# A late layernorm on ScalarE, mask work in three pieces, another order of q groups, and one attention step a unit later

## The chip, the cores and the metric

The kernel runs on one core of one Trainium2 chip. The metric is the device time of one execution in microseconds, the median of several runs. The kernel before took 277.28 us (three runs, 276.76 to 277.5).

The engines are named as in the profile: PE is TensorE (PEld its weight loads), DVE is VectorE, ACT is ScalarE, POOL is GpSimd, and SP is SyncE, which here issues the DMAs.

## The reference

One transformer block on a sequence of 2048 rows of width 640, in bf16: linear attention with a learned softmax feature map, then a gated feed-forward part. Layernorm has no scale and no bias.

```python
def _A_ref(x, wqkv, w_phi, wo):            # B, S, D = 1, 2048, 640;  H = 32 heads of Dh = 20
    q, k, v = ...                          # x @ wqkv, split into heads
    pq = jnp.einsum("bhsd,hdf->bhsf", q, w_phi)
    pk = jnp.einsum("bhsd,hdf->bhsf", k, w_phi)
    phi_q = jnp.concatenate([_softmax(pq), _softmax(-pq)], axis=-1)
    phi_k = jnp.concatenate([_softmax(pk), _softmax(-pk)], axis=-1)
    kv = jnp.einsum("bhsf,bhsd->bhfd", phi_k, v)
    z  = jnp.einsum("bhsf->bhf", phi_k)
    num = jnp.einsum("bhqf,bhfd->bhqd", phi_q, kv)
    den = jnp.einsum("bhqf,bhf->bhq", phi_q, z)[..., None] + 1e-6
    return (num / den).transpose(...).reshape(B, S, D) @ wo

def _B_ref(x, w_gate, w_up, w_down):       # F = 1536
    return (_gelu(x @ w_gate) * (x @ w_up)) @ w_down

h  = x + _A_ref(_layernorm(x), ...)
h2 = h + _B_ref(_layernorm(h), ...)
```

## The kernel before

**Tiles and batches.** The 2048 rows are 16 tiles of 128 rows (`t` = 0 to 15), in four batches `b` of four tiles. The width 640 is five chunks `c` of 128. PE's program order and SP's are those of the source; so are those of the other engines, each of which runs its own instructions in order and waits on semaphores for the others. A wait at the head of one engine's queue therefore holds all that stands behind it.

**The k and v phase** (source lines 411 to 505) goes over the tiles. For each tile: the layernormed rows, transposed, lie in `LN1T[b]` (640 columns on five chunks of partitions); `k_tile` multiplies them by Wk with the feature map already folded in (matrix `Wk2`, PSUM tile `pk`) and ACT makes the two exponentials, exp(pk) and exp(-pk), in `Ek[t]` (line 310); `v_mm` and `v_ev` make v for a tile four ahead (`vS`, a ring of eight; a column of ones beside v gives z). `k_norm` (line 313) normalises: DVE sums each head's exponentials (`sk`, line 317) and takes the reciprocal (`rs`, line 321); the two signs' `vt`, v times that reciprocal, are made on POOL (sign 1 always, sign 0 for the tiles of `VP` = 0, 2, 4, 6, 9, 11) and on DVE (sign 0 of the others, put off by one tile through `todo`). On DVE the order of one tile is thus sk(t), vt(t-1) where it is DVE's, rs(t). `kv_tile` multiplies `Ek` and `vt` into the accumulator `kvp`, 20 small matmuls a tile, in four batches: `KVG` = after the k matmuls of tiles 5, 9, 13 and 15; tiles 12 to 15 come last (lines 503 and 504). PSUM in this phase is three buffers of two banks and the two banks of `kvp`.

**Layernorm of tiles 0 and 1.** The first two tiles are handled apart: k and v are computed from the merely centred rows (`xc`), and the row factor rstd is put in by the scale operands of the exponentials and of the copy of v. Only q needs their full layernorm in `LN1T[0]`, so it is made late, in iteration 10: `ln_ap(0)` on DVE (line 144) and `ln_a(1)` on DVE (line 390), each followed by a DMA transpose on SP's queue (line 155). `ln_ap(t, on_act=True)` would make the same on ACT (line 139), which needs `mr`, the mean times minus rstd, which tile 0's statistics (`ln_0`) do not compute. SP's next issues after these two transposes are the loads of Wg, Wo and Wu in iteration 13 (lines 499 to 501).

**POOL's KV work.** In iteration 9, behind that tile's `vt`, POOL clears `KV` (line 489), builds the mask `kmask` of the head blocks (lines 490 to 495: a memset and four affine selects, each pair on one half of the partitions) and copies it into the two columns of `KV` that stand for z (lines 496 and 497). `KV` and `kmask` are wanted by `kv_mask`, after the last `kv_tile`: DVE and POOL multiply the accumulator by the mask into `KV` (line 355).

**The q phase.** q is computed transposed, 20 chunks of 128 columns by 512 rows, chunk number 5*b + c. `QG` lists how the chunks are grouped; a group of two fills one PSUM tile `pq` (`q_mm`, line 368, five matmuls of 512 columns a chunk) and ACT takes the two exponentials (`q_exp`, line 373). Four groups are done in iteration 15 of the k phase (`QT`), ahead of the last `kv_tile`s; the others in the order written out by hand in lines 739 to 781, between the attention steps of tiles 0 and 1. Attention of tile t wants the five chunks of its batch.

**Attention steps.** `attn_a` multiplies phi_q by KV (PSUM tiles `ab`, line 546, two PSUM buffers a tile) and copies the result out (`AB`, line 566, ACT or DVE); `attn_b`, `attn_b2`, `attn_b3` make the quotient (`pr`, `den`, `w` on POOL or DVE; `rd`, `tt`, `o` on DVE) and send `o` through a DMA transpose; `attn_c` multiplies by Wo (`po`, line 618); `attn_d`, `attn_d2`, `attn_e` add the residual, take the second layernorm and transpose it to `LN2T`.

**The feed-forward units.** From 90 us on a unit is `gate_up` (ten matmuls into one PSUM buffer `gu`, line 678; gelu on ACT, line 681; product `GT` on DVE, line 684) or `down` (`pd`, line 697). `weave(units, stages)` runs the units in order and puts each attention step in front of the unit whose number it was given; `attn_at(t, i, offs)` gives the eight steps of tile t the numbers i + offs. In the first weave, tile 3 has i = 1 and its `attn_a` stands in front of unit 2. PSUM is here four buffers of two banks, and a new tile takes the buffer that was released first in the source's order; `attn_a` copies its halves in the order (1, 0) for tile 5 and (0, 1) for the others, which sets which of its two buffers is released first.

Of the kernel before, what the change touches and what calls it, by code (L numbers as in the profile page):

```python
# [10 lines left out]
ALU = mybir.AluOpType  # L11
# [6 lines left out]
def kernel(  # L18
# [12 lines left out]
    nc = tc.nc  # L31
# [17 lines left out]
    LQ = (7, 8, 9, 9, 10)  # L49
    FQ = (10, 11, 12, 13, 14)  # L50

    QG = ((0, 1), (2, 3), (4, 5), (6,), (7, 8), (9, 10), (11, 12), (13, 14), (15,), (16,), (17,), (18,), (19,))
    QT = (15, 15, 15, 15)
    T3 = 3

# [20 lines left out]
    x_sb = [const.tile([P, 4, D], BF16, name=f"x_sb{b}") for b in range(NB)]  # L76
# [5 lines left out]

    Eq = [const.tile([P, len(g), 2, 512], BF16, name=f"Eq{j}") for j, g in enumerate(QG)]
    ident = const.tile([P, P], BF16, name="ident")
# [6 lines left out]
    def eq(t, c, s):  # L91
        for E, g in zip(Eq, QG):
            if t // 4 * NC + c in g:
                return E[:, g.index(t // 4 * NC + c), s, t % 4 * P:(t % 4 + 1) * P]

    def small(pool, shape, name, bufs=3):
        return pool.tile(shape, F32, name=name, bufs=bufs)

    def gtile(name):
        return psG.tile([P, 2, 512], F32, name=name, tag="G")  # L100

    def ln_stats(pool, tiles, tag, act=True, between=None, log=False):

        n = len(tiles)
        mv = small(pool, [P, n, nc.vector.BN_AGGR_DIM], "mv" + tag)
        stats = small(pool, [P, n, 2, nc.vector.BN_STATS_DIM], "stats" + tag)
        for j, xt in enumerate(tiles):
            for i in range(2):
                nc.vector.bn_stats(stats[:, j, i, :], xt[:, i * HD:(i + 1) * HD])
                if between and i == j == 0:  # L110
                    between()
        for j in range(n):
            nc.vector.bn_aggr(mv[:, j, :], stats[:, j])
        ve = small(pool, [P, n], "ve" + tag)
        rstd = small(pool, [P, n], "rstd" + tag)
        if log is not False:

            def root():
                nc.scalar.activation(ve, mv[:, :, 1], ACTF.Ln, bias=eps)
                nc.scalar.activation(rstd, ve, ACTF.Exp, scale=-0.5)  # L120

            if log is True:
                root()
            else:
                log.append(root)
        else:
            nc.gpsimd.tensor_scalar_add(ve, mv[:, :, 1], EPS)
            nc.gpsimd.tensor_tensor(rstd, ve, nhalf[:, 0:n], op=ALU.pow)

        mr = small(pool, [P, n], "mr" + tag)  # L130
        if act:
            for j in range(n):
                nc.gpsimd.tensor_scalar(mr[:, j:j + 1], mv[:, j, 0:1], rstd[:, j:j + 1], -1.0,
                                        op0=ALU.mult, op1=ALU.mult)
        return [(xt, mv[:, j, 0:1], rstd[:, j:j + 1], mr[:, j:j + 1]) for j, xt in enumerate(tiles)]
# [11 lines left out]
    def transpose_to(dst, src, on_pe, on_dve=False):  # L147

        if on_pe:
            tp = psG.tile([P, 16, P], BF16, name="tp", tag="G")  # L150
            for c in range(NC):
                nc.tensor.transpose(tp[:, c, :], src[:, c * P:(c + 1) * P], ident)  # L152
            (nc.vector.tensor_copy if on_dve else nc.scalar.copy)(dst, tp[:, 0:NC, :])  # L153
        else:
            nc.sync.dma_start_transpose(dst, src)
# [7 lines left out]
    p1 = p1_cm.__enter__()  # L163
# [81 lines left out]
    lnp, Ek, Vt = {}, {}, {}  # L245

    CT = (0, 1)
    nrstd = [p1.tile([P, 1], F32, name=f"nrstd{t}") for t in CT]

    def ln_0(t):  # L250
        xt, mean, rstd, _ = lnp[t] = ln_stats(p1, [x_sb[0][:, t, :]], f"c{t}", False, None, True)[0]
        nc.gpsimd.tensor_scalar(nrstd[t], rstd, -1.0, None, op0=ALU.mult)
        xc = fp.tile([P, D], BF16, name="xc", bufs=2)
        nc.vector.tensor_scalar(xc, xt, mean, None, op0=ALU.subtract)
        return xc
# [5 lines left out]
    def ln_ap(t, on_act=False, on_pe=False):  # L261
        ln = (ln_act if on_act else ln_dve)(p1, "1", *lnp[t])
        if on_pe:
            lnp[t] = ln
        else:
            transpose_to(LN1T[t // 4][:, :, t % 4 * P:(t % 4 + 1) * P], ln, False)
# [38 lines left out]
    def k_tile(t):  # L305
        pk = gtile("pk")
        proj(pk, t, Wk2, rows=t == 0)
        Ek[t] = ev.tile([P, 2, D], BF16, name="E", bufs=8)
        for s in range(2):
            nc.scalar.activation(Ek[t][:, s, :].rearrange("p (u f) -> p u f", u=2), pk[:, :, 0:HD],  # L310
                                 ACTF.Exp, scale=((lnp[t][2], nrstd[t]) if t in CT else (1.0, -1.0))[s])
# [47 lines left out]
    def q_mm(j, part=(0, 1)):  # L359

        if 0 in part:
            pqs[j] = gtile("pq")
        for i, bc in enumerate(QG[j]):
            if i not in part:
                continue
            b, c = divmod(bc, NC)
            for kc in range(NC):
                nc.tensor.matmul(pqs[j][:, i, :], lhsT=Wq2[:, kc, c * P:(c + 1) * P], rhs=LN1T[b][:, kc, :],  # L368
                                 start=(kc == 0), stop=(kc == NC - 1))

    def q_exp(j, signs=(0, 1)):
        for s in signs:
            nc.scalar.activation(Eq[j][:, :, s, :], pqs[j][:, 0:len(QG[j])], ACTF.Exp, scale=(1.0, -1.0)[s])  # L373

# [82 lines left out]
    for t in range(NT):  # L457
        if t == T3:
            ps_cm.close()
            psG = ps_cm.enter_context(tc.tile_pool(name="psG", bufs=3, space=PSUM, reuse_waits="tile"))  # L460
            psK = ps_cm.enter_context(tc.tile_pool(name="psK", bufs=1, space=PSUM, reuse_waits="tile"))
            kvp = psK.tile([P, 2, 512], F32, name="kvp")
        k_tile(t)
        if t == 0:
            ln_ap(6)
        if t in FQ:
            fold(WqT, Wq2, True, [i for i, f in enumerate(FQ) if f == t])
        for j in range(len(QT)):
            if t == QT[j]:
                q_mm(j)  # L470
                q_exp(j)
        for i in KVG.get(t, ()):
            kv_tile(i)
        if 0 < t < NT - 4:
            v_mm(t + 4)
        if t > 0 and t + 6 < NT:
            ln_ap(t + 6, on_act=True)
        if 0 < t < NT - 4:
            v_ev(t + 4)
        if t % 2 == 0 and t + 8 < NT:  # L480
            ln_st(t + 8, t + 9)
        k_norm(t)
        load_T(WqT, 0, *[i for i, f in enumerate(LQ) if f == t])
        if t == 10:

            ln_ap(0)
            transpose_to(LN1T[0][:, :, P:2 * P], ln_a(1), False)
        if t == 9:
            nc.gpsimd.memset(KV, 0.0)
            nc.gpsimd.memset(kmask, 1.0)  # L490
            for r in HALF:
                nc.gpsimd.affine_select(out=kmask[r], in_=kmask[r], pattern=[[4, NC], [-Dh, 4]],
                                        compare_op=ALU.is_ge, fill=0.0, base=0, channel_multiplier=1)
                nc.gpsimd.affine_select(out=kmask[r], in_=kmask[r], pattern=[[-4, NC], [Dh, 4]],
                                        compare_op=ALU.is_ge, fill=0.0, base=Dh - 1, channel_multiplier=-1)
            nc.gpsimd.tensor_copy(KV[:, :, 0, :, KC - 1], kmask)
            nc.gpsimd.tensor_copy(KV[:, :, 1, :, 0], kmask)
        if t == 13:
            nc.sync.dma_start(Wg, wg_v)
            nc.sync.dma_start(Wo, wo_v)  # L500
            nc.sync.dma_start(Wu, wu_v)
# [60 lines left out]
    def attn_a(t, dve=0):  # L562
        attn_a_mm(t)
        AB, ab = ABs[t % 2], st[t, "ab"]
        for u in ((1, 0) if t in (5,) else (0, 1)):
            (nc.vector.tensor_copy if u >= 2 - dve else nc.scalar.copy)(
                AB[:, :, u * UH:(u + 1) * UH].rearrange("p s h f -> p s (h f)"), ab[u][:, :, 0:UH * KC])
        st[t] = AB
# [169 lines left out]

    q_mm(q)
    attn_a(0, 1)  # L740
    q_exp(q)
    q_mm(q + 1)
# [41 lines left out]
    def attn_at(t, i, offs):  # L784

        fns = (attn_a, attn_b, attn_b2, attn_b3, attn_c, attn_d, attn_d2, attn_e)
        return [(i + o, fn, t) for fn, o in zip(fns, offs) if o >= 0]

    SHORT = (0, 2, 3, 4, 9, 9, 10, 12)
    SHORT2 = (0, 2, 3, 4, 10, 10, 11, 13)  # L790
    LONG = (0, 1, 2, 5, 5, 6, 7)

    def attn_rest(t, i):
# [2 lines left out]


    weave(gus(0, 0, 256) + downs(0, (0, 1)),
          attn_at(2, 0, (-1, 0, 1, 2, 7, 7, 8, 10)) + attn_at(3, 1, (1, 2, 3, 4, 9, 9, 10, 12)) + attn_at(4, 6, SHORT2) + attn_at(5, 9, SHORT2) +
          attn_at(6, 13, SHORT2))  # L800
    weave(gus(0, 256, 512) + downs(0, (2, 3)),
          attn_at(7, 0, SHORT) + [(12, split), (14, attn_pair, 8), (16, attn_pair, 10)] + attn_rest(8, 15) +
# [37 lines left out]
```

## Time and profile before

| | |
|---|---|
| median of the runs | 277.28 us (276.76 to 277.5) |
| profiled execution | 277.27 us |
| its span, first to last instruction | 275.5 us |
| granted TensorE clock | 1.000 |
| PE busy | 270.3 us (98%) |
| DVE busy | 175.7 us (64%) |
| ACT busy | 140.2 us (51%) |
| POOL busy | 97.1 us (35%) |
| weight loads (PEld) busy | 173.6 us (63%) |
| DVE busy between 30 and 60 us | 9.79 + 9.90 + 9.79 us of 30 |

The busy shares are means over stages. The k and v phase lies between about 6 and 70 us, the q phase between 59 and 89.5 us, the woven feed-forward part after that. Matmuls are pipelined and their ends are modelled, so a busy PE is not yet a PE at its peak, and the starts of neighbouring instructions are the better measure there. Spans on POOL are rough. A line of the timeline gives the start in us, the duration in us, the engine, the source line, the operation, what it writes and reads, how many instructions are merged in it, and in brackets the idle time before them with what ended it. A line of the waits gives who waited for whom, the total in us, how many times, and the longest.

### The profile page before, as it was taken

The numbers are of one execution on the slowest core, as the hardware profiler recorded it, in microseconds if no ns is written. First come the engines' busy times: TensorE is split into PE (matmuls) and PEld (weight loads), VectorE is DVE, ScalarE is ACT, GpSimd is POOL, SyncE is SP. The second block draws the span as 40 slices with busy tenths as digits, with TensorE's granted clock in tenths as the row PEclk, the third lists the DMA queues.
The fourth block names the chain that finished last, engine by engine and source line by source line (L and its number), as shares of the span: only waits on it lengthen the run. The fifth ranks groups of instructions, "written<-read, shape, count | busy, mean of one in ns | idle before, by whom it ended". The sixth has DMA issues, their size and how long they took to land.

```text
span 275.5 us, 5939 instructions
## 1 busy us (share of the span) xinstructions
PE 270.3 (98%) x2345; PEld 173.6 (63%) x2345; DVE 175.7 (64%) x333; ACT 140.2 (51%) x241; POOL 97.1 (35%) x218
## 2 busy tenths in 40 slices
PE   7999999999899999999999999999999999999995
PEld 4777777765455887788764545675455576444574
DVE  5889999999495776675478773356866333333322
ACT  5789898869489755374552345223245510223100
POOL 4248897765202317365312553101165300000000
DMA  7963525589820021323111142110123111000011
GB/s 197 209 230 61 75 51 101 83 266 394 264 91 0 4 48 38 84 48 77 26 48 48 26 69 51 38 61 2 48 47 71 27 48 50 24 0 0 0 50 48
DMA packets 42235, 21.37 MB, mean 78 GB/s; under 512 B 35040, under 2 KB 40416, under 8 KB 42208
## 3 DMA queue, kind: packets, MB, share of 16 engines
q1 hardware_dynamic: 41552, 20.98, 30.1%
q8 instruction: 18, 0.29, 0.5%
q10 hardware_dynamic: 656, 0.03, 0.2%
q14 instruction: 9, 0.07, 0.1%
HBM read 10.18 MB, written 2.62 MB: 46 GB/s over the span
## 4 chain that ended last, share of the span: by engine, by line
PE 86%; issue 4%; DVE 4%; DMA 2%; ACT 1%; POOL 1%; SPq 0%; DVEq 0%; ACTq 0%; POOLq 0%
PE gu L678 37%; PE pd L697 19%; PE po L618 8%; PE pv L277 6%; PE pk L277 5%; PE pq L368 5%; PE ab L546 2%; DMA Wv<-in_A_wqkv_dram 2%; DVE sk L317 2%; DVE rs L321 1%; PE kvp L343 1%; PE tp L152 1%; POOL vt L325 1%; PE pv L293 1%; PE wa L232 1%
## 5 line engine op out<-in xcount | busy, mean ns | idle before, releaser
L681 ACT ACTIVATE g<-gu 128x512 bf16<-128x512 f32 (+1 forms) x60 | 30.7, 512 | 68.9 <-PE gu L678 68.7
L684 DVE TENSOR_TENSOR GT<-gu,g 128x512 bf16<-128x512 f32 (+1 forms) x60 | 34.5, 580 | 47.8 <-PE gu L678 39.2
L678 PE MATMUL gu<-LN2T,Wg 128*128 128x512 bf16 (+1 forms) x300 | 61.8, 337 | 0.0
L678 PE MATMUL gu<-LN2T,Wu 128*128 128x512 bf16 (+1 forms) x300 | 61.8, 337 | 0.0
L697 PE MATMUL pd<-Wd,GT 128*128 128x320 bf16 (+2 forms) x396 | 53.5, 295 | 0.0
L697 PEld LDWEIGHTS <-GT 128*128 128x128 bf16 x396 | 37.9, 98 | 14.7 <-DVE GT L684 0.2
L678 PEld LDWEIGHTS <-Wu 128*128 128x128 bf16 x300 | 29.4, 98 | 22.6
L678 PEld LDWEIGHTS <-Wg 128*128 128x128 bf16 x300 | 28.8, 98 | 21.4
L277 PEld LDWEIGHTS <-LN1T 128*128 128x128 bf16 x290 | 27.8, 98 | 10.5
L700 DVE TENSOR_TENSOR y<-pd,x_sb 128x320 bf16<-128x320 f32 (+2 forms) x29 | 13.9, 480 | 28.9 <-PE pd L697 28.9
L325 POOL TENSOR_TENSOR vt<-vS,rs 128x672 bf16<-128x672 bf16 x22 | 29.1, 1343 | 9.1 <-DVE rs L321 8.8
L618 PE MATMUL po<-Wo,oT 128*128 128x320 bf16 x160 | 24.3, 299 | 0.0
L277 PE MATMUL pk<-Wk,LN1T 128*128 128x320 bf16 x160 | 24.2, 299 | 0.0
L368 PE MATMUL pq<-LN1T,Wq 128*128 128x512 bf16 x100 | 23.1, 379 | 0.0
L317 DVE TENSOR_REDUCE sk<-E 128x64 f32<-128x1280 bf16 x16 | 22.9, 1430 | 0.0
L373 ACT ACTIVATE Eq<-pq 128x1024 bf16<-128x1024 f32 (+1 forms) x26 | 20.0, 830 | 1.7 <-PE pq L368 1.7
L618 PEld LDWEIGHTS <-oT 128*128 128x128 bf16 x160 | 15.6, 98 | 7.4 <-ACT oT L153 0.5
L310 ACT ACTIVATE E<-pk 128x640 bf16<-128x640 f32 x28 | 18.2, 707 | 3.8 <-PE pk L277 3.8
L277 PE MATMUL pv<-Wv,LN1T 128*128 128x320 bf16 x130 | 19.8, 299 | 0.0
L595 DVE TENSOR_TENSOR tt<-AB,w 128x1280 bf16<-128x1280 f32 x12 | 17.8, 1486 | 1.1 <-POOL w L588 0.9
L139 ACT ACTIVATE ln<-x_sb,v,rstd 128x640 bf16<-128x640 bf16 x14 | 12.9, 920 | 10.4 <-POOL v L657 10.0
L368 PEld LDWEIGHTS <-Wq 128*128 128x128 bf16 x100 | 9.4, 98 | 10.0
(114 smaller groups left out, 292.8 us busy)
## 6 DMA issues: line engine op xcount, KB each, us to landing
out_dram<-y SPq DMA_DIRECT2D x15, 160.0 KB, 1.8
Wg<-in_B_w_gate_dram SPq DMA_DIRECT2D x1, 1920.0 KB, 7.9
Wu<-in_B_w_up_dram SPq DMA_DIRECT2D x1, 1920.0 KB, 12.8
Wd<-in_B_w_down_dram SPq DMA_DIRECT2D x1, 1920.0 KB, 7.9
x_sb<-in_A_x_dram SPq DMA_DIRECT2D x2, 640.0 KB, 6.3
Wo<-in_A_wo_dram SPq DMA_DIRECT2D x1, 800.0 KB, 9.5
x_sb<-in_A_x_dram SPq DMA_DIRECT2D x4, 160.0 KB, 3.4
Wv<-in_A_wqkv_dram SPq DMA_DIRECT2D x2, 320.0 KB, 4.6
```

What stands on the lines that cost most here:

```text
L277: nc.tensor.matmul(ps[:, u, 0:HD], lhsT=lnT(t, c), rhs=W[:, c, u * HD:(u + 1) * HD], start=(c == 0), stop=(c == NC - 1))
L310: nc.scalar.activation(Ek[t][:, s, :].rearrange("p (u f) -> p u f", u=2), pk[:, :, 0:HD], ACTF.Exp, scale=((lnp[t][2], nrstd[t]) if t in C ...
L317: nc.vector.reduce_sum(sk, Ek[t].rearrange("p s (h f) -> p (s h) f", f=Dh), axis=AX.X)
L325: eng.tensor_tensor(vt[:, s], vS[t % 8], rs[:, s * H:(s + 1) * H, None].to_broadcast([P, H, VC]), ALU.mult)
L368: nc.tensor.matmul(pqs[j][:, i, :], lhsT=Wq2[:, kc, c * P:(c + 1) * P], rhs=LN1T[b][:, kc, :], start=(kc == 0), stop=(kc == NC - 1))
L373: nc.scalar.activation(Eq[j][:, :, s, :], pqs[j][:, 0:len(QG[j])], ACTF.Exp, scale=(1.0, -1.0)[s])
L595: nc.vector.tensor_tensor(tt.rearrange("p s (h f) -> p s h f", f=Dh), num, w[:, :, :, None].to_broadcast([P, 2, H, Dh]), ALU.mult)
L618: nc.tensor.matmul(pos[u], lhsT=st[t][:, c, :], rhs=Wo[:, c, u * HD:(u + 1) * HD], start=(c == 0), stop=(c == NC - 1))
L678: nc.tensor.matmul(gu[i][:, 0:n], lhsT=W[:, c, f * P:(f + 1) * P], rhs=LN2T[b][:, c, a0:a1], start=(c == 0), stop=(c == NC - 1))
L681: nc.scalar.activation(g[:, 0:n], gu[0][:, 0:n], ACTF.Gelu_apprx_tanh)
L684: nc.vector.tensor_tensor(st[b, "g", f][:, a0:a1], gu[1][:, 0:n], g[:, 0:n], ALU.mult)
L697: nc.tensor.matmul(ps, lhsT=st[b, "g", f][:, tl * P:(tl + 1) * P], rhs=Wd[:, f, f0:f1], start=(f == 0), stop=(f == NF - 1))
```

## The change

It has five edits.

- The first group of `QG` becomes (5, 6), two chunks of batch 1; (4,) stands alone in its place. There are still 13 groups, and the four groups of iteration 15 still hold chunks 0 to 6.
- `ln_0` makes `mr` for tile 0 on POOL, and `ln_ap(0)` moves from DVE in iteration 10 to ACT in iteration 12. In the order of instructions it stands on ACT behind the Wq copy of iteration 12 and ahead of tile 13's exponentials. On SP tile 1's transpose comes first and tile 0's second; both still stand ahead of Wg, Wo and Wu.
- POOL's KV work is split: the two memsets in iteration 7, the four selects in iteration 8, the two copies in iteration 10, each behind that tile's `vt`.
- In `attn_a` the copy order (1, 0) is for tile 4 and no longer for tile 5.
- `attn_a`, `attn_b`, `attn_b2` and `attn_b3` of tile 3 come one unit later; its `attn_a` now stands behind unit 2's `gate_up`. Its later steps stay.

```diff
-    QG = ((0, 1), (2, 3), (4, 5), (6,), (7, 8), ...)
+    QG = ((5, 6), (0, 1), (2, 3), (4,), (7, 8), ...)
...
     def ln_0(t):
-        xt, mean, rstd, _ = lnp[t] = ln_stats(p1, [x_sb[0][:, t, :]], f"c{t}", False, None, True)[0]
+        xt, mean, rstd, mr = lnp[t] = ln_stats(p1, [x_sb[0][:, t, :]], f"c{t}", False, None, True)[0]
         nc.gpsimd.tensor_scalar(nrstd[t], rstd, -1.0, None, op0=ALU.mult)
+        if t == 0:
+            nc.gpsimd.tensor_scalar(mr, mean, nrstd[0], None, op0=ALU.mult)
...
         if t == 10:
-            ln_ap(0)
             transpose_to(LN1T[0][:, :, P:2 * P], ln_a(1), False)
-        if t == 9:
+        if t == 12:
+            ln_ap(0, on_act=True)
+        if t == 7:
             nc.gpsimd.memset(KV, 0.0)
             nc.gpsimd.memset(kmask, 1.0)
+        if t == 8:
             for r in HALF:
                 nc.gpsimd.affine_select(out=kmask[r], in_=kmask[r], ...)
                 nc.gpsimd.affine_select(out=kmask[r], in_=kmask[r], ...)
+        if t == 10:
             nc.gpsimd.tensor_copy(KV[:, :, 0, :, KC - 1], kmask)
             nc.gpsimd.tensor_copy(KV[:, :, 1, :, 0], kmask)
...
-        for u in ((1, 0) if t in (5,) else (0, 1)):
+        for u in ((1, 0) if t in (4,) else (0, 1)):
...
-          attn_at(2, 0, (-1, 0, 1, 2, 7, 7, 8, 10)) + attn_at(3, 1, (1, 2, 3, 4, 9, 9, 10, 12)) + ...
+          attn_at(2, 0, (-1, 0, 1, 2, 7, 7, 8, 10)) + attn_at(3, 1, (2, 3, 4, 5, 9, 9, 10, 12)) + ...
```

More of the change, by code (lines that the diff above doesn't have):

```diff
@@ L50 @@
     FQ = (10, 11, 12, 13, 14)
-    QG = ((0, 1), (2, 3), (4, 5), (6,), (7, 8), (9, 10), (11, 12), (13, 14), (15,), (16,), (17,), (18,), (19,))
+    QG = ((5, 6), (0, 1), (2, 3), (4,), (7, 8), (9, 10), (11, 12), (13, 14), (15,), (16,), (17,), (18,), (19,))
     QT = (15, 15, 15, 15)
@@ L798 @@
     weave(gus(0, 0, 256) + downs(0, (0, 1)),
-          attn_at(2, 0, (-1, 0, 1, 2, 7, 7, 8, 10)) + attn_at(3, 1, (1, 2, 3, 4, 9, 9, 10, 12)) + attn_at(4, 6, SHORT2) + attn_at(5, 9, SHORT2) +
+          attn_at(2, 0, (-1, 0, 1, 2, 7, 7, 8, 10)) + attn_at(3, 1, (2, 3, 4, 5, 9, 9, 10, 12)) + attn_at(4, 6, SHORT2) + attn_at(5, 9, SHORT2) +
           attn_at(6, 13, SHORT2))
```

## The prediction

> **What bounds the kernel now.** I read the page's chain first, then who waited for whom on TensorE (PE), then the timeline around each of its stalls. The granted clock is 1.000 in the core view, so no part of this is a clock matter.
>
> ```profile
> PE 86%; issue 4%; DVE 4%; DMA 2%; ACT 1%; POOL 1%; SPq 0%; DVEq 0%; ACTq 0%; POOLq 0%
> ```
>
> The chain is PE almost throughout, so the ceiling of any scheduling edit is the time that PE stands still. The waits of PE name all of it:
>
> ```profile
> PE wu L214 <- PEq L824: 0.8, 1, 0.8
> PE kvp L343 <- POOL vt L325: 0.7, 1, 0.7
> PE pv L293 <- DMA Wv<-in_A_wqkv_dram: 0.5, 1, 0.5
> ```
>
> The first and third lie before 7 us and nothing in the diff reaches them. The second is the one at stake. Timeline around it (start, us, engine, line):
>
> ```profile
> 66.87 2.29 PE L343 MATMUL kvp<-vt,E 128*64 128x84 bf16 x110
> ...
> 67.79 0.86 DVE L325 TENSOR_TENSOR vt<-vS,rs 128x672 bf16<-128x672 bf16 x1
> 67.86 1.96 POOL L325 TENSOR_TENSOR vt<-vS,rs 128x672 bf16<-128x672 bf16 x1 [1.35 <-DVE rs L321]
> 69.87 0.38 PE L343 MATMUL kvp<-vt,E 128*64 128x84 bf16 x10 [0.71 <-POOL vt L325]
> ...
> 70.19 2.33 PE L368 MATMUL pq<-LN1T,Wq 128*128 128x512 bf16 x10
> ```
>
> PE's last ten phi_k@V matmuls wait for tile 15's second vt on POOL, done at 69.82. Matmul ends are modelled, so I size the stall by starts: 80 kvp matmuls took 42.00 to 43.66 (1.66), 40 took 30.14 to 31.03 (0.89), so 40 more cost 0.77 and these 120 should take 2.43; they took 66.87 to 70.19, 3.32. The stall is 0.89.
>
> Why POOL is late: from about 41 us on VectorE (DVE) runs sk, vt, rs for each tile with no idle time, tile 15's sk starting at 64.95 though its E was ready at 60.84. So any DVE time before 67 us moves the 69.82. The dear piece of that queue:
>
> ```profile
> 49.76 2.58 POOL L325 TENSOR_TENSOR vt<-vS,rs 128x672 bf16<-128x672 bf16 x2 [1.32 <-DVE rs L321]
> ...
> 51.53 1.81 DVE L144 TENSOR_SCALAR ln<-x_sb,mvc,rstdc 128x640 bf16<-128x640 bf16 x1
> ...
> 52.28 0.83 POOL L489 MEMSET KV<- 128x880 bf16 x1
> ...
> 53.27 0.43 DVE L390 TENSOR_SCALAR ln<-x_sb,va 128x640 bf16<-128x640 bf16 x1
> ...
> 53.62 1.47 DVE L317 TENSOR_REDUCE sk<-E 128x64 f32<-128x1280 bf16 x1
> ...
> 54.70 1.31 POOL L325 TENSOR_TENSOR vt<-vS,rs 128x672 bf16<-128x672 bf16 x1
> 55.01 1.72 DVE L325 TENSOR_TENSOR vt<-vS,rs 128x672 bf16<-128x672 bf16 x1
> ```
>
> The ln of tile 0 takes 1.81 here; the seven other L144 take 0.44 to 0.45. It finishes 1.00 after POOL's vt and 0.23 after the memset. DVE's vt at 55.01 takes 1.72 against 0.85 when POOL is idle, and ends 0.72 after POOL's vt; those at 45.09, 60.45, 63.66 and 66.30 end 0.71 to 0.72 after POOL's too. So such DVE operations stand still while POOL works, and POOL's KV work (52.28 to 54.70) both stretched ln 0 and pushed vt of tile 10 to 54.70.
>
> The second, smaller stall is in the first gate/up units:
>
> ```profile
> 92.34 0.56 PE L546 MATMUL ab<-KV,Eq 64*128 64x88 bf16 x20
> ...
> 92.47 0.42 DVE L684 TENSOR_TENSOR GT<-gu,g 128x256 bf16<-128x256 f32 x1 [0.63 <-ACT g L681]
> ...
> 92.95 0.71 PE L678 MATMUL gu<-LN2T,Wg 128*128 128x256 bf16 x5
> ```
>
> From ab to the next gu is 0.61 here, 0.49 or 0.50 at 89.56, 97.41 and 102.65: 0.11 lost, because the gu of unit 2 reuses the PSUM buffer of unit 0, whose GT ends at 92.90.
>
> **The change, part by part.**
>
> *ln of tile 0 to ScalarE (ACT).* Off DVE: one operation, 1.81 less the overlap of about 0.07 at its end, 1.74. On ACT: one of the L139 kind, 0.92. By the order of instructions it stands after the Wq copy that ends at 54.53 and ahead of tile 13's E, which moves from 54.40 to about 55.3. The cover is ACT's 1.43 idle before 57.75 (waiting for tile 14's pk), which shrinks to about 0.5, so tile 14's E stays. Tile 13's E ends at 56.6, and DVE wants it only at 59.11, or 57.1 if DVE is 2.0 early. PE's PSUM buffers released by that E and the Wq copy behind it are wanted at 57.55 and 57.87, freed at about 56.6 and 57.2. Cost nothing; with the cover gone, up to 0.92 less 0.65 of slack. The new `mr` on POOL (0.26 in most rows of L133) falls in POOL's idle time from 5.62 to 8.29: nothing.
>
> *Transposes on SP.* Tile 1's goes first, tile 0's after ACT at about 55.5 (before: 53.41 and 54.72); Wg, Wo and Wu queue behind and start about 0.7 later, Wo landing near 67 and wanted at 79.26, Wg and Wu wanted at 90.05. Nothing. The landing takes 2.6 at the median and 4.3 at most: 58.1 to 59.8 for tile 0, with the first q matmul at 59.23.
>
> *q group (5, 6) in front.* It reads batch 1 and takes 2.16 or so, so batch 0 is wanted at 61.4: this covers the transposes, 1.6 at least. Without it up to 0.6 would be exposed. Seven chunks in four groups stay; the last exp still ends at 68.82, with ab of tile 0 at 72.45.
>
> *POOL's KV work in three pieces.* The memsets (0.94) go behind tile 7's vt at 45.77, into 1.35 of idle POOL time. The four selects (0.29 apart, 1.16) go behind tile 8's vt at 48.44, into 1.32 of idle time. The two copies (0.30) go behind tile 10's vt. So tile 10's vt on POOL may start at 52.30 instead of 54.70. What each piece does to DVE is not shown in the trace; bounds by the nearest rows:
> - memset KV against DVE's vt of tile 7 (queued at 45.09): nothing, if it slips in as POOL's vt ends, to 0.94, if it waits as L144 waited. I take nothing: L144 is another form.
> - selects against DVE's vt of tile 8: nothing (L390 kept its 0.43 with two selects running beside it) to 1.1 (behind all four). I take nothing, as the row is about selects. If POOL's selects wait instead, POOL is 0.5 later.
> - ln of tile 1 (L390), queued at 51.53 while POOL works through tile 9's second vt, with tile 10's vt ready behind it: it slips in at 52.34 and ends at about 52.65, or waits through tile 10's vt (53.61) and ends at 53.9, or through the copies too (53.95) and ends at 54.25. Before it ended at 53.69.
>
> Carried to tile 11's rs (start 56.65 before). Slips in: sk 11 to 54.05, POOL's vt 10 to 53.96, DVE's vt 10 0.72 behind, rs at 54.6: 2.0 early. Waits for one vt: sk to 55.3, vt 10 now unhindered (0.85), rs at 55.97: 0.7 early. Waits for the copies too: 0.35 early. With POOL 0.5 later from the selects: 1.5, 0.2 or 0.15 late. From there the queue shifts as one, since each E is ready at least 2.0 before its sk. PE gains the smaller of that and 0.89.
>
> On who waits, the row is L144: queued at 51.53, it did not get in as POOL's vt ended at 52.34, but after the memset. One row, and with a memset behind, not a vt; I weigh the two orders alike and take slipping in, as it alone leaves the stall wholly covered.
>
> The Trainium skill ("SBUF — State Buffer", Who interferes with whom) says that whichever was issued first gets the port shared by VectorE and GpSimd for the whole instruction, and that a Vector operation with two SBUF inputs is held only by GpSimd operations that read SBUF. By it L390 would slip in and the memset would cost vt of tile 7 nothing, a full gain; L144's row speaks against its first half, and by that row alone the gain at PE would be 0.35 to 0.7.
>
> *ab of tile 3 a unit later.* Unit 2 then takes a buffer that DVE's copy of tile 2 freed at 91.05, and ab of tile 3 (at 93.34) the one of unit 0 (92.90). PE gains 0.11. Behind it: tile 3's AB copies move 1.0 later, its o to about 100.2 and its transpose lands near 103, wanted at 104.25; po of tile 2 now reuses unit 5's buffer, whose GT moves ahead of tile 3's tt to about 98.3, wanted at 98.9. Nothing, but 0.6 of cover. The swapped copy order of tiles 4 and 5 keeps each buffer's release ahead of its use by over 1.
>
> **Sum.** Profiled execution 277.27 (span 275.5, 1.77 around it; the median of the runs is 277.28). Less 0.89, less 0.11: 276.27, so 276.3.
>
> **The rivals.**
> - *The ln of tile 1 takes ln 0's place* as the operation that waits behind POOL. For: L144's row. Against: it is one operation, and the vt of tile 10 becomes free. Gain 0.15 to 0.7 plus 0.11: 276.5 to 277.0.
> - *The change doesn't bring the chain forward at all:* selects push POOL by 0.5 and L390 waits through vt and copies. 277.2 to 277.4.
> - *Slower: DVE loses every turn to POOL*, at tiles 7, 8 and 10. Place: DVE's vt of tile 8 behind all four selects, 48.44 to 50.2, 1.1 late. Then POOL's vt of tile 9 end at 53.4, L390 at 55.0 to 55.4, rs of tile 11 0.35 to 0.75 late; with the memset in front up to 0.9 more. It decides as soon as L390 ends later than about 54.6, since then rs of tile 11 is later than before. 277.5 to 278.5. Against: L390 beside the selects.
>
> **How the numbers follow.** Slips in 0.50, the ln of tile 1 waits 0.25, nothing gained 0.10, slower 0.15. Range: 276.27 less 0.35 for the spread of the runs (276.76 to 277.5), 275.9, up to 277.4, which leaves out the slower case. Within 0.3% (what a measurement of this kernel can tell from no change) is 276.45 to 278.11. The first case lies only 0.2 under that bound: 0.45 of its 0.50 faster; the second gives 0.05. Faster 0.50. Of the slower case a third lies over 278.11 and I add 0.05 for a margin I misjudged (po of tile 2, pk of tile 15): slower 0.10. Same 0.40.
>
> **What would show it.** Right: PE's wait of kvp on vt is gone, L390 takes 1.1 or so, tile 10's vt on POOL starts before 53, tile 15's vt ends before 68.9, ab to gu of unit 3 is 0.50. Wrong: L390 over 2.0; DVE's vt of tile 7 or 8 over 1.5; kvp still waiting; or a PE wait for pk, po or pq that was not there.

## The result and the profile after

The changed kernel takes 276.67 us (median of 22 runs, 276.28 to 276.86), the kernel before 277.04 us over its 22 runs (276.42 to 278.08). The ratio is 0.9982, 95% interval 0.9975 to 0.9990: 0.50 us faster, between 0.28 and 0.69. The forecast was 1.0 us. The direction was right and so was the mechanism; by the ratio half of the size arrived, by the medians 0.37 us. The time lies within the 0.3% band of 276.45 to 278.11 us, which the prediction had given 0.40, and not under it, which it had given 0.50. The profiled execution after took 276.69 us with a span of 274.7 us, so 1.99 us lie outside the span; before it was 277.27 and 275.5, so 1.77.

First the chain of the profile after, which answers to the chain shown of before:

```profile
PE 95%; DMA 2%; ACT 1%; DVE 1%; SPq 0%; issue 0%
```

PE went from 86% to 95%: the detour of the chain through DVE's and POOL's sk, rs and vt is gone. The waits of PE no longer hold kvp on vt; among those of PE's weight loads there is one that was not there before:

```profile
PE wu L214 <- PEq L828: 0.8, 1, 0.8
PE pv L295 <- DMA Wv<-in_A_wqkv_dram: 0.5, 1, 0.5
...
PEld L279 <- DMA LN1T<-ln: 0.4, 1, 0.4
```

The timeline after, around tile 1's ln (line 390 is 392 here, 325 is 327):

```profile
47.45 1.31 POOL L327 TENSOR_TENSOR vt<-vS,rs 128x672 bf16<-128x672 bf16 x1 [0.52 <-DVE rs L323]
48.72 0.86 POOL L495 TENSOR_SCALAR_AFFINE_SELECT kmask<-kmask 64x20 bf16<-64x20 bf16 x1
...
48.55 0.93 DVE L327 TENSOR_TENSOR vt<-vS,rs 128x672 bf16<-128x672 bf16 x1
...
51.78 1.31 POOL L327 TENSOR_TENSOR vt<-vS,rs 128x672 bf16<-128x672 bf16 x1
...
51.86 1.42 DVE L392 TENSOR_SCALAR ln<-x_sb,va 128x640 bf16<-128x640 bf16 x1
...
53.05 1.40 POOL L327 TENSOR_TENSOR vt<-vS,rs 128x672 bf16<-128x672 bf16 x1
54.40 0.27 POOL L500 COPY KV<-kmask 128x20 bf16<-128x20 bf16 x1
...
54.59 0.84 DVE L327 TENSOR_TENSOR vt<-vS,rs 128x672 bf16<-128x672 bf16 x1
```

Two turns are to be seen. DVE's vt at 48.55 waited for POOL's vt (ended 48.76) and went next: it took 0.93 and POOL's first select, queued behind, took 0.86 in place of 0.22 to 0.23. Tile 1's ln at 51.86 waited for POOL's vt (ended 53.09), ended at 53.28, and POOL's next vt took 1.40 in place of 1.31. So DVE slips in when the running POOL operation ends, though POOL's next one is ready. Tile 10's vt then costs DVE 0.84 in place of 1.72.

Around the last kvp and the first ab steps of the woven part:

```profile
66.51 0.86 DVE L327 TENSOR_TENSOR vt<-vS,rs 128x672 bf16<-128x672 bf16 x1
66.58 1.97 POOL L327 TENSOR_TENSOR vt<-vS,rs 128x672 bf16<-128x672 bf16 x1 [1.35 <-DVE rs L323]
67.06 2.48 PE L345 MATMUL kvp<-vt,E 128*64 128x84 bf16 x120
...
69.47 1.84 PEld L370 LDWEIGHTS <-Wq 128*128 128x128 bf16 x10
```

```profile
92.72 0.57 PE L550 MATMUL ab<-KV,Eq 64*128 64x88 bf16 x20
93.22 0.72 PE L682 MATMUL gu<-LN2T,Wg 128*128 128x256 bf16 x5
```

The last vt ends at 68.55 and the 120 kvp matmuls run without a break, 2.41 from their start to the next q matmul (3.32 before). From ab to the next gu is 0.50 (0.61 before).

The new loss is early. Before tile 6's statistics DVE waits for x, and the transposed rows of tile 6 then reach PE late:

```profile
16.80 0.89 DVE L109 BATCH_NORM_STATS2 stats<-x_sb 128x6 f32<-128x320 bf16 x2 [0.97 <-DMA x_sb<-in_A_x_dram]
...
20.52 1.52 PE L279 MATMUL pk<-Wk,LN1T 128*128 128x320 bf16 x10
22.08 1.12 PE L279 MATMUL pv<-Wv,LN1T 128*128 128x320 bf16 x7
```

From pk to pv is 1.56 here where ten such matmuls take 1.36: 0.20 lost. In the profile of before that wait for x was shorter:

```profile
16.47 0.89 DVE L109 BATCH_NORM_STATS2 stats<-x_sb 128x6 f32<-128x320 bf16 x2 [0.62 <-DMA x_sb<-in_A_x_dram]
```

The change does not touch this load. Its landing differs from one execution to the next, of the same kernel too, as the second profiles below show, and that turned out to be the key to the size.

### The profile page after: what moved, and what is told of

The parts are those of the page before. It is cut to its first block, busy times and chain, and to the rows that moved or that the text cites. A ratio compares the mean times of both kernels' runs of the same rounds, so it can differ in the third digit from the quotient of the medians.

```text
span 274.7 us, 5928 instructions
## 1 busy us (share of the span) xinstructions
PE 269.5 (98%) x2332; PEld 173.5 (63%) x2345; DVE 173.9 (63%) x332; ACT 141.0 (51%) x242; POOL 97.3 (35%) x219
## 4 chain that ended last, share of the span: by engine, by line
PE 95%; DMA 2%; ACT 1%; DVE 1%; SPq 0%; issue 0%
PE gu L682 38%; PE pd L701 19%; PE pk L279 8%; PE po L622 8%; PE pq L370 8%; PE pv L279 7%; PE ab L550 3%; PE kvp L345 2%; DMA Wv<-in_A_wqkv_dram 2%; PE wa L232 1%; PE tp L152 1%; PE pv L295 1%; ACT vS L299 1%; DVE LN1T L153 0%; SPq L181 0%
```

## The experiments

Theory: DVE's queue decides, together with POOL's turns, and both the late layernorm and the split of the KV work are needed. First rival: only the number of DVE operations counts. Second rival, formed on the way: the stall is set by when DVE's queue starts, and that differs from one execution to the next.

### One part at a time

Tile 0's layernorm on ScalarE, and the q group in front:

```diff
-    QG = ((0, 1), (2, 3), (4, 5), (6,), ...)
+    QG = ((5, 6), (0, 1), (2, 3), (4,), ...)
...
-        xt, mean, rstd, _ = lnp[t] = ...
+        xt, mean, rstd, mr = lnp[t] = ...
...
+        if t == 0:
+            nc.gpsimd.tensor_scalar(mr, mean, nrstd[0], None, op0=ALU.mult)
...
         if t == 10:
-            ln_ap(0)
...
+        if t == 12:
+            ln_ap(0, on_act=True)
```

> The kernel before with two of the edits alone: tile 0's layernorm on ScalarE in iteration 12, and the q group of tiles 5 and 6 in front. GpSimd's KV work stays whole in iteration 9. Theory of this study (a VectorE operation that waits gets in when the running GpSimd operation ends, and the KV work must leave iteration 9 too): tile 1's ln (line 390's operation) still waits for tile 9's second vt, 52.34, or for the KV memset, 53.1; GpSimd's vt of tile 10 still starts at about 54.7 behind the KV work, so VectorE's vt of tile 10 still ends at about 56.7, and TensorE's wait of kvp on vt stays at 0.6 to 0.9 us: time within 0.1 us of before. Rival (only the number of VectorE operations counts): 1.7 us fewer on VectorE, the wait is gone, 0.5 to 0.9 us faster.

Measured: 277.01 us (276.39 to 277.54), ratio 0.9993 (0.9980 to 1.0007). No difference that can be told, as the theory said; but in the profile the wait of kvp on vt was gone, which it had not said. The timeline:

```profile
50.74 1.82 DVE L392 TENSOR_SCALAR ln<-x_sb,va 128x640 bf16<-128x640 bf16 x1
...
53.87 0.84 DVE L327 TENSOR_TENSOR vt<-vS,rs 128x672 bf16<-128x672 bf16 x1
...
53.91 3.25 POOL L327 TENSOR_TENSOR vt<-vS,rs 128x672 bf16<-128x672 bf16 x2
```

Tile 1's ln waits through vt and the KV memset as tile 0's did before (1.82). But then DVE's vt of tile 10 was queued at 53.87, 0.04 ahead of POOL's (53.91), and got its turn first: it took 0.84, and POOL's two took 3.25 in place of 2.59. That wins 0.66 on the whole queue in this profile (table below), not 0. The rest of the loss is missing because this execution's queue started early, as the table shows.

The KV work in three pieces:

```diff
-        if t == 9:                 # memsets, selects and copies together
+        if t == 7:                 # memsets
+        if t == 8:                 # selects
+        if t == 10:                # copies
```

> The kernel before with GpSimd's KV work in three pieces (iterations 7, 8 and 10) as the only edit; tile 0's layernorm stays on VectorE in iteration 10. Theory of this study (who waits gets in at the next end): VectorE's ln of tile 0 gets in when tile 9's second vt ends, 53.1, then GpSimd's vt of tile 10, which waited, gets in before the ln of tile 1, which ends at about 55.0; sk of tile 11 starts 1.3 us later than before, but VectorE's vt of tile 10 no longer waits: rs of tile 11 about 0.4 us later than before, TensorE's wait of kvp on vt 1.1 to 1.3 us, 0.2 to 0.5 us slower. Rival (the KV work in front of tile 10's vt was the whole delay): rs of tile 11 is 0.9 us earlier, the wait is gone, 0.5 to 0.9 us faster.

Measured: 276.89 us (276.37 to 277.65), ratio 0.9996 (0.9981 to 1.0012). Neither is to be seen, though the interval, which reaches 0.33 us slower, does not shut out the low end of the theory's 0.2 to 0.5. The profile decides: the queue is 53.33 long in place of 53.35 (table below). The turns are as the theory had them, with tile 0's ln let in at the end of tile 9's second vt and tile 1's only after tile 10's:

```profile
51.17 1.43 DVE L144 TENSOR_SCALAR ln<-x_sb,mvc,rstdc 128x640 bf16<-128x640 bf16 x1
52.52 1.43 DVE L390 TENSOR_SCALAR ln<-x_sb,va 128x640 bf16<-128x640 bf16 x1
```

Both wait, and tile 1's ln ends at 53.95, not at 55.0. Of the 1.05 between them, 0.59 is that DVE's work on tile 6 started at 15.88 in this execution and at 16.47 in the one from which the expectation was worked out. Counted from there, rs of tile 11 starts 0.03 earlier than before (56.03 against 56.65), where 0.4 later was expected.

Phi_q@KV of tile 3 a unit later:

```diff
-        for u in ((1, 0) if t in (5,) else (0, 1)):
+        for u in ((1, 0) if t in (4,) else (0, 1)):
-          ... attn_at(3, 1, (1, 2, 3, 4, 9, 9, 10, 12)) ...
+          ... attn_at(3, 1, (2, 3, 4, 5, 9, 9, 10, 12)) ...
```

> The kernel before with phi_q@KV of tile 3 a unit later and the copy order (1, 0) for tile 4 in place of tile 5 as the only edits. Theory of this study: ab to the next gu goes from 0.61 to 0.50 us, nothing else, 0.11 us faster, which is under what five rounds tell; the wait of kvp on vt stays. Rival (a later buffer release takes it back): the time is the same or slower and a wait of po or gu on VectorE or ScalarE shows between 97 and 112 us.

Measured: 276.92 us (276.36 to 278.66), ratio 0.9991 (0.9971 to 1.0010); under what the runs can tell. Its profiled execution began late (278.66 us; PE waited 1.2 us for Wv), but the step itself is plain: from ab at 94.94 to gu at 95.44, 0.50, as in the changed kernel, and PE has no wait of po or gu.

The changed kernel without the q group in front:

```diff
-    QG = ((5, 6), (0, 1), (2, 3), (4,), ...)
+    QG = ((0, 1), (2, 3), (4, 5), (6,), ...)
```

> The changed kernel with the q groups in their old order, (0, 1) first and (4, 5), (6,) last of the four. Theory of this study (the group in front covers the late transpose of tile 0): the first q matmul, at about 59.4 us, waits for that transpose, issued at about 55.6 and landing 2.6 to 4.3 us later: 0 to 0.5 us of TensorE standing still, so 0 to 0.5 us slower than the changed kernel. Rival (the transpose always lands in time): the same time as the changed kernel, and no wait at the first q matmul.

Measured: 277.25 us (276.65 to 277.91), ratio to the kernel before 1.0010 (0.9995 to 1.0024). The first q matmul stands still:

```profile
57.87 1.52 PE L279 MATMUL pk<-Wk,LN1T 128*128 128x320 bf16 x10
59.74 2.54 PE L370 MATMUL pq<-LN1T,Wq 128*128 128x512 bf16 x11 [0.35 <-ACT Wq L241]
```

```profile
52.31 4.26 SPq L155 DMA_TRANSPOSE LN1T<-ln  x2
```

From pk to pq is 1.87 in place of 1.36: 0.51. The profile puts part of the wait down to the copy of Wq, but that copy stands where it stood: it starts 1.07 after pk in both kernels (58.94 here, 59.12 in the changed kernel), and in the changed kernel, whose first q group needs the same chunks of Wq, the first q matmul started at 59.41 while the copy was still running. The second of the two transposes ends its issue at 56.57, so begins near 55.4, and at the longest landing of that profile, 4.2, lands near 59.6. So the group in front is no ornament: without it the late layernorm costs about what the rest brings.

### The queue and its start

Both kernels were run once more as they stand.

> The kernel before as it stands, for a second execution in profile. Theory: the time from tile 6's first statistics to the end of the last vt is 53.3 to 53.4 us again, and TensorE's loss at the last kvp is that start less the start of TensorE's first v matmul less 9.0 us, or zero. Rival (the loss is a fixed 0.89 us): 0.8 to 0.9 us whatever these two starts are.

> The changed kernel as it stands, for a second execution in profile. Theory: the time from tile 6's first statistics to the end of the last vt is 51.7 to 51.8 us again, no loss at the last kvp unless tile 6's statistics start more than 10.6 us behind the first v matmul, and a loss at tile 6's v matmul (about 22 us) of that distance less 10.0 us, or zero. Rival (the 0.20 us at tile 6's v matmul is a fixed cost of the change): it shows again with the same size.

Measured: 276.41 us and 276.68 us. In the second profile of the kernel before, kvp runs from 66.71 to the next q matmul at 69.31, 2.60: only 0.18 lost, where 0.89 were lost in the first.

```profile
66.71 2.67 PE L343 MATMUL kvp<-vt,E 128*64 128x84 bf16 x120
...
69.31 0.76 PEld L368 LDWEIGHTS <-Wq 128*128 128x128 bf16 x5
```

The first statistics of tile 6, in the second profile of the kernel before and in that of the changed kernel:

```profile
15.60 0.88 DVE L109 BATCH_NORM_STATS2 stats<-x_sb 128x6 f32<-128x320 bf16 x2
```

```profile
16.89 0.89 DVE L109 BATCH_NORM_STATS2 stats<-x_sb 128x6 f32<-128x320 bf16 x2 [1.11 <-DMA x_sb<-in_A_x_dram]
```

So the kernel before waited 0.62 for this load in its first profile and not at all in its second; the changed kernel waited 0.97 and 1.11.

The table sets all profiles side by side. *Start* is the start of tile 6's first statistics on DVE less the start of PE's first v matmul. *Queue* is the time from there to the end of the last vt on POOL. *PE late* is how much later than 60.29 after its first v matmul PE reached the last kvp batch. The loss worked out is start + queue - 62.35 - PE late, or zero; the constant 62.35 is set by the first row. The loss measured is the time from that batch to the next q matmul less 2.43.

| kernel | start | queue | PE late | loss worked out | measured |
|---|---|---|---|---|---|
| before | 9.89 | 53.35 | 0.01 | 0.88 | 0.89 |
| before, again | 9.18 | 53.35 | 0.00 | 0.18 | 0.18 |
| KV pieces only | 9.18 | 53.33 | 0.08 | 0.08 | 0.08 |
| tile 3 only | 10.83 | 53.36 | 1.67 | 0.17 | 0.18 |
| mr only | 9.18 | 53.33 | 0.01 | 0.15 | 0.15 |
| before, x early | 9.18 | 53.35 | 0.17 | 0.01 | 0.02 |
| two memsets fewer | 9.18 | 53.35 | 0.48 | 0 | 0 |
| ln only | 9.18 | 52.69 | 0.01 | 0 | 0 |
| changed | 10.24 | 51.75 | 0.21 | 0 | 0 |
| changed, again | 10.45 | 51.74 | 0.40 | 0 | 0 |
| two memsets more | 9.18 | 51.74 | 0.00 | 0 | 0 |
| four memsets more | 10.39 | 51.75 | 0.35 | 0 | 0 |
| changed, old q order | 9.30 | 51.73 | 0.62 | 0 | 0 |
| changed, x early | 9.19 | 51.73 | 0.43 | 0 | 0 |

The queue is a constant of the program, to 0.03: 53.33 to 53.36 before, 51.73 to 51.75 after. The parts do not add up: the KV pieces alone win 0.02, the layernorm alone 0.66, both 1.60. The start is what varies: 9.18 when x comes in time, up to 10.45 in an ordinary execution (10.83 in the one that began late). In the kernel before, each 0.1 us of start over 9.00 is 0.1 us of loss, as long as PE itself is not late. In the changed kernel there is none at kvp, but in its three profiles with a late start PE is late at tile 6, in all by about the start less 10.04 (0.20, 0.41 and 0.35 worked out, with the 10.04 fitted to them; 0.21, 0.40 and 0.35 measured). The gain inside the span at a given start, worked out from the table, is thus the start less 9.00, at most 1.04, and the 0.11 of tile 3: 0.29 at 9.18, 1.00 at the 9.89 of the first profile.

PE can be late for other reasons too. The 0.62 of the old q order holds the 0.51 at the first q matmul. With two memsets fewer, most of the 0.48 is a wait at 27.71 for another tile's transposed rows, though the start was 9.18:

```profile
27.71 1.53 PE L277 MATMUL pv<-Wv,LN1T 128*128 128x320 bf16 x10 [0.31 <-DMA LN1T<-ln]
```

If the start matters so much, an earlier load of x should help:

```diff
     st_act(1, 1)
+    nc.scalar.dma_start(x_sb[1][:, 2:4, :], x_v[:, 6:8, :])
...
-    nc.sync.dma_start(x_sb[1][:, 2:4, :], x_v[:, 6:8, :])
```

> The changed kernel with one more edit: the load of tiles 6 and 7 of x is issued from ScalarE's queue right after the second statistics step of tile 1 (at about 8.2 us) and no longer from SyncE's queue behind the transposes of Wk (11.5 us). Theory (VectorE's queue runs without a gap from tile 6's statistics to the last vt, and that start is set by this load, which lands at another time in each execution): VectorE's wait for x ahead of tile 6's statistics goes, TensorE's wait for tile 6's transposed rows at about 22 us goes, and the time lies at the low end of the changed kernel's runs, 276.3 us, 0.3 to 0.4 us faster than its median, provided that the loads of Wv and Wk ahead of it are not slowed. Rival (the load's landing does not matter to the changed kernel, whose chain has slack): 276.6 to 276.8 us as without the edit.

> The kernel before with the same earlier load of tiles 6 and 7 of x as the only edit. Theory (that landing sets the start of VectorE's queue, whose length from tile 6's first statistics to the end of the last vt stays 53.35 us): the last vt ends 0.4 to 0.9 us earlier, TensorE's wait of kvp on vt shrinks to 0 to 0.2 us, the spread of the runs (276.4 to 278.2) closes from above, and the median falls to 276.4 to 276.6 us, 0.5 to 0.7 us faster than before, with none of the change's edits. Rival (the wait of kvp on vt comes from the work in iterations 9 and 10 alone): the wait stays at 0.7 to 0.9 us and the time at 277.1 us.

Measured: in the changed kernel 277.17 us (276.42 to 278.61), ratio to before 1.0007 (0.9990 to 1.0024); in the kernel before 276.95 us (276.74 to 277.21), ratio 0.9994 (0.9982 to 1.0006). Both miss their time. In the second the mechanism came as expected: DVE does not wait for x, the start is 9.18, the loss at kvp 0.02, and the runs close from above. But the first v matmul starts at 7.11 in place of 6.58:

```profile
7.11 1.79 PE L293 MATMUL pv<-Wv,LN1T 128*128 128x320 bf16 x12 [1.03 <-DMA Wv<-in_A_wqkv_dram]
```

What was won at 69 us was paid at 7 us in this execution, as the load of Wv was later here and in that of the changed kernel (7.00), where a later transpose was waited for as well, 0.4 us at 31.88:

```profile
PE pv L295 <- DMA Wv<-in_A_wqkv_dram: 0.9, 1, 0.9
...
PE pv L279 <- DMA LN1T<-ln: 0.4, 1, 0.4
```

That the earlier load itself delays Wv is not shown, and in these two executions it cannot have held it up on the way: x was issued only at 9.49 and 9.62 us, after Wv had landed. A late first v matmul also occurs without this edit (7.14 with tile 3 only, 6.80 with four memsets more). Yet the lowest of the twelve runs in the kernel before is 276.74, where the kernel before as it stands reached 276.42 in the same set, so something seems to be paid in every run. What that is stays open.

### The time outside the span

The changed kernel has 1.99 us outside its span on the mean of 22 runs; the kernel before 1.72 to 1.74 in each set of its runs. These 0.26 us come off the gain, and the forecast did not have them.

One GpSimd operation more:

```diff
 def ln_0(t):
+    if t == 0:
+        nc.gpsimd.tensor_scalar(mr, mean, nrstd[0], None, op0=ALU.mult)
```

> The kernel before with one GpSimd operation more: mr of tile 0 (mean times minus rstd), which nothing reads. It asks where the time outside the span comes from, which is 1.72 us on the mean in the kernel before and 1.99 us in the changed one. If the added GpSimd operation is the cause: 1.9 to 2.0 us outside the span. If it is the layernorm on ScalarE or the order of the transposes: 1.72 us. In both cases the span is that of before, 274.7 to 276.5 us.

Measured: 1.73 us outside the span; 277.52 us (276.43 to 278.36), ratio 1.0012 (0.9993 to 1.0031). Not the cause. Nor is the KV split (1.73) or tile 3 (1.73); the layernorm alone has 1.89. What that edit takes away is one DVE instruction, so DVE instructions were added to the changed kernel, and taken away from the kernel before without the edit:

```diff
 two and four more, in the changed kernel
-    for i in range(8):
+    for i in (0, 1, 0, 1, 2, 3, 4, 5, 6, 7):
+    for i in (0, 1, 2, 3, 0, 1, 2, 3, 4, 5, 6, 7):
         nc.vector.memset(vS[i][:, :, Dh], 1.0)
 two fewer, in the kernel before
-        nc.vector.memset(vS[i][:, :, Dh], 1.0)
+        (nc.vector if i < 6 else nc.gpsimd).memset(vS[i][:, :, Dh], 1.0)
```

> The changed kernel with two more VectorE instructions in its idle time before 3 us (two of the memsets of vS's ones columns are issued twice), which brings VectorE's count back to that of the kernel before. It asks what makes the time outside the span longer (1.99 us in the changed kernel, 1.73 us before). If VectorE's number of instructions does: 1.73 us outside the span, an unchanged span of about 274.7 us at the median, and 276.4 us, 0.25 us faster than the changed kernel. If the layernorm on ScalarE or the order of SyncE's transposes does: 1.9 to 2.0 us outside the span and 276.7 us.

> The kernel before with two of VectorE's eight early memsets issued on GpSimd, so that VectorE has as few instructions as in the changed kernel. If VectorE's number of instructions sets the time outside the span: 1.9 to 2.0 us there. If not: 1.73 us. The span is that of before in both cases (274.7 to 276.5 us).

> The changed kernel with four more early memsets on VectorE in place of two. VectorE's instruction count is then two above that of the kernel before. So far two kernels with the lower count had 1.95 to 1.99 us outside the span and those with the higher one 1.73 to 1.75. If the time outside falls with every VectorE instruction more: about 1.5 us. If it is a step or repeats with the count: 1.7 us or about 2.0 us. The span stays that of the changed kernel, 274.3 to 275 us at the median, with 51.74 us from tile 6's first statistics to the end of the last vt.

Measured, with DVE's instruction count from the page's engine rows:

| kernel | DVE instructions | outside the span, mean | median | ratio to before |
|---|---|---|---|---|
| before, two memsets fewer | 331 | 1.95 | 277.30 | 0.9996 (0.9980 to 1.0011) |
| changed | 332 | 1.99 | 276.67 | 0.9982 (0.9975 to 0.9990) |
| before | 333 | 1.73 | 277.04 | |
| changed, two memsets more | 334 | 1.75 | 276.52 | 0.9971 (0.9950 to 0.9992) |
| changed, four memsets more | 336 | 1.65 | 276.50 | 0.9978 (0.9965 to 0.9991) |

By these counts the padded kernels have one and three DVE instructions more than the kernel before, where their expectations said as many and two more, and the kernel with two memsets fewer has one less than the changed kernel, where its expectation said as many.

In these five kernels the time outside the span goes with the number of DVE instructions: fewer make it longer, and two useless memsets in DVE's idle first microseconds bring 0.24 us of it back. With four, 1.65 lies between the two cases of the expectation, 1.5 and 1.7. The number is not all that counts: three more kernels with 332 have 1.89 (layernorm alone), 1.94 (old q order) and 1.95 (changed, x early), against the 1.99 of the changed kernel. Why is not shown, as no profile looks outside the span.

That the whole time follows is not shown either. With two memsets fewer, 0.22 us more lie outside, and the median is 277.30 against 277.29 us of the kernel before in the same set of runs. Both padded kernels beat the kernel before; that they beat the changed one too is what 276.5 against 276.67 suggests, but they were timed in other sets, in which the kernel before itself had medians from 276.82 to 277.29, and the intervals overlap.

## Why the prediction was right, and where its size was off

- **The stall at the last kvp goes.** Right. The range of the queue was put at 2.0 us early at best and 1.5 with POOL pushed by its selects; it is 1.60 (53.35 to 51.75). POOL's selects did wait, 0.63, for DVE's vt of tile 8. Of the signs named, kvp no longer waits and tile 15's vt ended at 68.55, before 68.9; tile 10's vt on POOL started at 53.05, not before 53, in an execution whose queue started 0.33 later than the first.
- **Who gets in.** The choice was between L144's row, in which a waiting ln stayed out at the end of a vt, and slipping in. It slips in, with a vt behind it, though L390 then took 1.42 and not 1.1 or so. With a memset behind it, it stayed out again in the layernorm-only kernel (1.82). The split memset cost DVE's vt of tile 7 nothing (it ended 0.72 after POOL's vt, as before). So of the Trainium skill's two rules ("SBUF — State Buffer", Who interferes with whom) the second is borne out by that vt. The first says who holds the port; that the one queued first also goes next is what the prediction made of it. That holds here against a vt and a select, but not against a memset, where the ln ended 0.23 to 0.24 after the memset and not right after the vt.
- **The layernorm on ScalarE and the q group in front cost nothing.** Right, and the cover had a price of 0.51 where up to 0.6 was said.
- **Tile 3: 0.11.** Right, 0.61 to 0.50.
- **The term that was mis-sized: the stall of 0.89, taken as that of every execution.** It was read from one execution, and it is start less 9.00: the second execution of the same kernel lost 0.18. The one that was read lay 0.23 us over the median of the kernel before. The queue's start is set by x's landing, which the row of tile 6's statistics showed as a wait of 0.62 for a DMA; the prediction looked for what PE waits for and not for what DVE's queue had waited for at its head. In the span the medians differ by about 0.6 in place of 1.0, 275.3 (277.04 less 1.73) to 274.7, which lies between the 0.29 worked out for a start of 9.18 and the 1.00 for 9.89.
- **What stays open there.** How often each start occurs in executions without a profile is not shown. With the load at its old place, the seven profiles without the whole change started at 9.18 (five times), 9.89 and 10.83, and the five with it at 9.18, 9.30, 10.24, 10.39 and 10.45. A late start costs the changed kernel 0.2 to 0.4 at tile 6. Of the change only `mr` runs before 17 us, and the two kernels that have `mr` without the KV pieces (layernorm alone, mr only) started at 9.18, so chance is the likelier reading; that the change makes late starts more frequent is not ruled out.
- **What was not in the sum at all:** 0.26 us outside the span. Taken from the 0.6 inside it, that leaves the 0.37 by which the medians differ.
- **The rivals.** That tile 1's ln takes tile 0's place behind POOL is what the layernorm-only kernel does, where the queue still became 0.66 shorter. That the chain does not come forward at all is refuted by the 1.60. That DVE loses every turn did not happen in any profile.

## What to carry to other kernels

A stall read from one profile is a difference of two arrivals; before it is put into a sum, find what sets each of the two, and if one of them hangs on a DMA landing, measure a second execution or carry the range. An engine whose queue runs without a gap for 50 us hands a late start on to its end, so the piece to watch is the last wait at its head. Edits around two engines that take turns need not add up: 0.02 and 0.66 us one by one, 1.60 together. And the order of the work behind them can decide whether the gain is kept: without the q group in front, 0.51 of it was lost again.

## What the runs showed of the hardware that was not expected

- The time outside the span differs from program to program: 1.95 us with 331 VectorE instructions, 1.89 to 1.99 with 332, 1.73 with 333, 1.75 with 334 and 1.65 with 336, every run within 0.2 us of its kernel's mean. What sets it is not known.
- A VectorE operation that waited for a running GpSimd operation went next when that one ended, ahead of GpSimd's own next, ready one (vt 0.93, ln 1.42); the GpSimd operation that was passed over took longer, a select 0.86 in place of 0.22 or 0.23, a vt 1.40 in place of 1.31. With a memset as GpSimd's next, the ln did not get in before it (1.81 and 1.82).
- The same load, issued at the same place, was waited for by VectorE for 0.62 us in one execution of the kernel before and not at all in the next.
